# One chunk per turn, and seven products for blocks 2 and 3 too, in a fused recurrence and two-layer kernel

## Chip, cores, metric

One core of one Trainium2 chip (trn2). The metric is device time in microseconds, the median of several executions. "Span" is the time from the first to the last instruction in the profile; the device time of an execution is 1.7 to 3.3 us longer than its span.

## The reference

```python
f = lower_bound + (1 - lower_bound) * sigmoid(f_logit)      # [4, 6144, 256]
for t in range(6144):
    h = f[:, t] * h + (1 - f[:, t]) * x[:, t];  y[:, t] = h
h1, h2 = y @ w1, y @ w2                                     # 24576 tokens, 256 -> 1024
out = maximum(h1, h2) @ w_out                               # 1024 -> 256
```

Results are float32. The kernel works in fp16 with float32 accumulation.

## The kernel before

Tokens are cut into 48 *blocks* of 512. Blocks 0 to 3 are fetched singly and turned (transposed) by TensorE. All later tokens come in *chunks* of 1024, two blocks: GpSimd's queue fetches a chunk of f and of x into scratch memory in HBM, converted to fp16, and the sync queue then transposes the scratch into SBUF by DMA. Chunk p+2 feeds *pair* p (blocks 2p and 2p+1), p = 2 to 23.

Per block there are a gate (sigmoid, ScalarE), decay, drive and two scans (VectorE), then two layers. The maximum is written h1 + relu(h2 − h1), so the *first layer* is y · (w2 − w1) with a ReLU (16 matmuls 512 wide, ScalarE's ReLU after each four), and the *second layer* contracts 8 pieces of the ReLU with w_out and 2 pieces of y with w1·w_out: 40 matmuls 256 wide. From pair 2 on, the second layer of two blocks is one product of 2 x 2 quarters and is done with seven products instead of eight: 140 matmuls 128 wide, at the price of four sums on VectorE. These products of pair p−1 run between the first-layer matmuls of pair p.

```python
def cross(*cs):                       # transposes of one or more chunks, then the next fetch
    if len(cs) > 1:                   # wait until the last chunk is in scratch
        nc.sync.dma_start(out=seen[:], in_=scratch[1][cs[-1] % NSCR][CH - 1 : CH, 0:16])
    for c in cs:
        for s in range(2):            # f, x
            dst = inpool.tile([P, KC, CH], HALF, name=("fT", "xT")[s])
            nc.sync.dma_start_transpose(out=dst[:], in_=scratch[s][c % NSCR][:])
            held[c, s] = dst
    pool_waits(held[cs[-1], 0][:, 0, 0:1])     # a one-column copy on GpSimd
    if cs[-1] + 1 < NCHUNK:
        for s in range(2):
            fetch(cs[-1] + 1, s)
# ... cut ...
# sevenths(p), all pairs but the last: 7 products of 20 matmuls, banks X, B, E in PSUM
product("X", part(0, 0), plain(0, lo), True);  then(seed("B", "X"))       # ScalarE copies X to B
product("E", sub(1), given(t1), True);         then(snapshot("E", 5))
product("X", sub(2), given(t2));               then(snapshot("X", 2))
product("B", part(0, 1), plain(1, lo));        then(leave("B", ja, lo, None, False))  # ScalarE
product("X", sub(3), given(t3));               then(leave("X", jb, hi, 5, False))     # VectorE adds
product("E", sub(4), plain(1, hi));            then(leave("E", ja, hi, 2, True))      # VectorE adds
product("X", part(1, 1), given(t4));           then(leave("X", jb, lo, None, True))   # X again
# ... cut: steps for blocks 0 and 1 ...
        cross(4, 5)
        # block 0's second layer, turn(2), gate(2), block 1's first layer, then
        turn(turn_steps(3));  gate(3);  early = scan_steps(3)
        for fc in range(FC):                    # block 2, beside block 1's second layer
            first_layer(2, fc);  second_layer(1, fc)
            if fc < 4: early[fc]()
        cross(6)
        for fc in range(FC):                    # block 3, beside block 2's second layer
            first_layer(3, fc);  second_layer(2, fc)
            # gates, decay, drive, scans of pair 2 in between
        for p in range(PAIR0, NPAIR):           # 16 slots a pair
            # block 3's second layer beside pair 2; sevenths(p - 1) from pair 3 on
            if slot == 2 and p + 3 < NPAIR:
                cross(blocks[2 * p + 6][3])
```

Of the kernel before, what the change touches and what calls it, by code (L numbers as in the profile page):

```python
# [14 lines left out]
P = 128  # L15
# [3 lines left out]
def kernel(  # L19
# [123 lines left out]

    def cross(*cs):


        if len(cs) > 1:
            nc.sync.dma_start(
                out=seen[:], in_=scratch[1][cs[-1] % NSCR][CH - 1 : CH, 0:16]
            )  # L150
        for c in cs:
            for s in range(2):
                dst = inpool.tile([P, KC, CH], HALF, name=("fT", "xT")[s])
                nc.sync.dma_start_transpose(out=dst[:], in_=scratch[s][c % NSCR][:])
                held[c, s] = dst
        pool_waits(held[cs[-1], 0][:, 0, 0:1])
        if cs[-1] + 1 < NCHUNK:
            for s in range(2):
                fetch(cs[-1] + 1, s)

# [160 lines left out]
    lbc = const.tile([P, KC], FP32)  # L321
    seen = const.tile([1, 16], HALF)
    waited = const.tile([P, 1], FP32)
# [200 lines left out]
    def sevenths(p):  # L524
# [12 lines left out]
        def then(fn):  # L537
            steps[-1][-1] = fn
# [69 lines left out]
        def given(t):  # L608
            return lambda k: t[:, k, :]

        product("X", part(0, 0), plain(0, lo), True)
        then(seed("B", "X"))
        product("E", sub(1), given(t1), True)
# [16 lines left out]
        else:  # L630
            product("X", sub(2), given(t2))
            then(snapshot("X", 2))
            product("B", part(0, 1), plain(1, lo))
            then(leave("B", ja, lo, None, False))
            product("X", sub(3), given(t3))
# [28 lines left out]
    with tc.manual_schedule():  # L664
# [11 lines left out]
        )  # L676
        for c in range(1, 6):
            for s in range(2):
                fetch(c, s)
# [39 lines left out]
        for step in scan_steps(1):  # L719
            step()  # L720
        cross(4, 5)
        for fc in range(FC):
# [8 lines left out]
        for step in scan_steps(2):  # L731
            step()
        for step in make_sevens():
            step()
        for fc in range(2, FC):
            first_layer(1, fc)
            if fc == 3:
                second_layer(0, 7)
        turn(turn_steps(3))
        gate(3)  # L740
        early = scan_steps(3)
        for fc in range(FC):
            first_layer(2, fc)
            second_layer(1, fc)
            if fc < 4:
                early[fc]()
        cross(6)
        scans = {PAIR0: pair_scans(PAIR0)}
        gates = {0: 0, 1: 1, 4: 2, 5: 3}
        order = {  # L750
            2: ("decay0", "drive0"),
            3: ("scan00",),
            4: ("scan01",),
            6: ("decay1",),
            7: ("drive1",),
        }
        for fc in range(FC):
            first_layer(3, fc)
            second_layer(2, fc)
            if fc in gates:  # L760
                pair_gate(PAIR0, gates[fc])
            for t in order.get(fc, ()):
                scans[PAIR0][t]()

        queue, due = [], 0
        pieces3, piece = (1, 3, 5, 9, 11, 13, 15), 0
        for p in range(PAIR0, NPAIR):
            first = p == PAIR0
            more = p + 1 < NPAIR
            seq = [  # L770
                (27, scans[p]["scan10"]),
                (36, scans[p]["scan11"]),
                (112, lambda: sum3(p)),
            ]
            if more:
                scans[p + 1] = pair_scans(p + 1)
                seq += [
                    (64, scans[p + 1]["decay0"]),
                    (66, scans[p + 1]["drive0"]),
                    (70, scans[p + 1]["scan00"]),  # L780
                    (84, scans[p + 1]["scan01"]),
                    (131, scans[p + 1]["decay1"]),
                    (133, scans[p + 1]["drive1"]),
                ]
            if not first:
                seq += [
                    (9, lambda: sum1(p - 1)),
                    (18, lambda: sum2(p - 1)),
                    (50, lambda: sum4(p - 1)),
                ]  # L790
                queue += sevenths(p - 1)
            seq.sort(key=lambda e: e[0])
            gates = {4: 0, 6: 1, 12: 2, 14: 3} if more else {}
            for slot in range(2 * FC):
                first_layer(2 * p + slot // FC, slot % FC)
                if first and slot in pieces3 or p == PAIR0 + 1 and slot == 1:
                    second_layer(2 * PAIR0 - 1, piece)
                    piece += 1
                if p > PAIR0 + 1 or (p == PAIR0 + 1 and slot >= LAG):
                    due += NSEV / (2 * FC)  # L800
                    while due >= 1:
                        due -= 1
                        queue.pop(0)()
                if slot == 2 and p + 3 < NPAIR:
                    cross(blocks[2 * p + 6][3])
                if slot in gates:
                    pair_gate(p + 1, gates[slot])
                while seq and seq[0][0] < (slot + 1) * 9:
                    seq.pop(0)[1]()
# [38 lines left out]
```

## Time and profile before

| | |
|---|---|
| median, range | 379.66 us, 379.19 to 379.68 |
| span | 377.7 us |
| TensorE, VectorE, ScalarE busy | 97%, 90%, 80% |
| a pair in the steady state | 14.70 us, all of it TensorE; VectorE 14.0 |
| loop fetch, transpose, fetch | 14.6 us a chunk (mean between transposes, chunks 8 to 25) |

A group of lines in the profile carries the source line of a helper: L441/L435 is the first layer, L650/L647/L651 the seven products, L487/L481 the plain second layer, L506/L500 the sums, L230/L225 the scans, L285/L280 the gates, L568/L562 an addition that empties a PSUM bank, each first in the kernel before and then in the changed one.

### The profile page before, as it was taken

The page shows a single profiled execution, that of the slowest core. Times are in us where ns is not written, and L with a number is a line of the kernel's source. Part 1 is how long each engine was busy: PE and PEld are TensorE (multiplying, and loading weights), DVE is VectorE, ACT ScalarE, POOL GpSimd, SP SyncE. Part 2 cuts the span into 40 slices and gives each one's busy share as a digit, 9 for nine tenths or more (in the row PEclk, how much of TensorE's full clock was granted, in tenths as well). Part 3 has the DMA queues.
Part 4 walks back from the last instruction along what each step waited for, and adds up shares of the span by engine and source line. Part 5 has one row for each costly group of instructions (what it writes and reads, how often), then busy time and mean ns, then how long its engine had stood idle before and what let it go on. Part 6 is the DMA issues. An engine that isn't in the chain of part 4 may idle for free.

```text
span 377.7 us, 9593 instructions
## 1 busy us (share of the span) xinstructions
PE 367.9 (97%) x4136; PEld 279.8 (74%) x4136; DVE 338.7 (90%) x410; ACT 302.4 (80%) x410; POOL 35.6 (9%) x79
## 2 busy tenths in 40 slices
PE   5999999999999999999999999999999999999994
PEld 3777767777777777777777777777777777777784
DVE  4796789999999999999999999999999999999772
ACT  5865897888888798888888887887988888889752
POOL 1500101110101101101201201011011001010000
PEclk9999999999999999999999999999999999999999
DMA  7996979998999999999999899999899899980223
GB/s 254 246 223 131 309 143 214 227 193 189 273 134 257 223 184 266 222 184 225 203 200 301 208 161 254 147 247 274 132 263 279 134 241 221 185 282 3 112 113 114
DMA packets 104813, 77.17 MB, mean 204 GB/s; under 512 B 93570, under 2 KB 95618, under 8 KB 104066
## 3 DMA queue, kind: packets, MB, share of 16 engines
q1 hardware_dynamic: 101538, 51.19, 60.5%
q0 software_dynamic: 2544, 25.17, 34.7%
q8 instruction: 32, 0.52, 0.6%
q10 hardware_dynamic: 688, 0.20, 0.2%
q14 instruction: 11, 0.09, 0.1%
HBM read 53.48 MB, written 48.23 MB: 269 GB/s over the span
## 4 chain that ended last, share of the span: by engine, by line
PE 94%; DVE 3%; DMA 1%; issue 0%; SPq 0%; ACT 0%; DVEq 0%
PE ps L650 44%; PE dT L441 43%; PE ps L487 5%; DMA osb<-in_x_dram 1%; DVE S L506 1%; PE ps L180 1%; DVE r L230 1%; DVE r L264 1%; PE ps L397 0%; DVE v L223 0%; DVE osb L568 0%; DVE osb L496 0%; PE ps L137 0%; DVE osb L589 0%; PE ps L383 0%
## 5 line engine op out<-in xcount | busy, mean ns | idle before, releaser
L449 ACT ACTIVATE r<-dT 128x1024 f16<-128x1024 f32 x192 | 195.9, 1023 | 53.4 <-PE dT L441 53.2
L441 PE MATMUL dT<-r,wd 128*128 128x512 f16 x768 | 225.5, 379 | 0.4 <-DVE r L230 0.2
L650 PEld LDWEIGHTS <-S 128*128 128x128 f16 x1760 | 115.5, 101 | 37.6 <-issue 0.5
L650 PEld LDWEIGHTS <-r 128*128 128x128 f16 x1320 | 90.9, 101 | 36.8 <-issue 0.2
L230 DVE TENSOR_TENSOR_SCAN r<-ff,r,v 128x512 f16<-128x512 f16 x88 | 108.2, 1269 | 0.8
L650 PE MATMUL ps<-t,S 128*128 128x128 f16 x1320 | 101.6, 219 | 0.0
L506 DVE TENSOR_TENSOR S<-r 128x2560 f16<-128x2560 f16 x44 | 65.3, 1485 | 14.5 <-ACT r L449 14.4
L441 PEld LDWEIGHTS <-wd 128*128 128x128 f16 x768 | 67.6, 113 | 5.2 <-DVE wd L365 1.2
L650 PE MATMUL ps<-wob,r 128*128 128x128 f16 x704 | 69.9, 219 | 0.0
L506 DVE TENSOR_TENSOR S<-r,S 128x2560 f16<-128x2560 f16 x44 | 64.8, 1473 | 0.0
L285 ACT ACTIVATE u<-fT 128x512 f16<-128x512 f16 x88 | 56.0, 637 | 1.3 <-DMA fT<-scr 1.3
L213 DVE TENSOR_SCALAR ff<-u,nom 128x512 f16<-128x512 f16 (+1 forms) x98 | 31.5, 344 | 8.5 <-ACT u L285 3.7
L650 PE MATMUL ps<-w,r 128*128 128x128 f16 x176 | 38.5, 219 | 0.0
L348 POOL CAST waited<-fT 128x1 f32<-128x1 f16 x21 | 8.8, 418 | 282.8 <-DMA fT<-scr 282.8
L650 PE MATMUL ps<-t,r 128*128 128x128 f16 x430 | 34.1, 219 | 0.1
L568 DVE TENSOR_TENSOR osb<-ps,sn 128x512 f32<-128x512 f32 x44 | 30.1, 683 | 3.2 <-PE ps L650 3.2
L650 PE MATMUL ps<-wob,S 128*128 128x128 f16 x352 | 32.6, 219 | 0.0
L223 DVE TENSOR_TENSOR v<-u,xT 128x1024 f16<-128x1024 f16 x44 | 30.0, 682 | 0.0
L556 ACT COPY sn<-ps 128x512 f32<-128x512 f32 x44 | 25.8, 587 | 2.4 <-PE ps L650 2.4
L566 ACT COPY osb<-ps 128x512 f32<-128x512 f32 x43 | 25.0, 582 | 0.8 <-PE ps L650 0.8
L487 PEld LDWEIGHTS <-r 128*128 128x128 f16 x160 | 16.0, 101 | 6.6
L650 PE MATMUL ps<-w,S 128*128 128x128 f16 x88 | 19.3, 219 | 0.0
(58 smaller groups left out, 131.9 us busy)
## 6 DMA issues: line engine op xcount, KB each, us to landing
out_dram<-osb SPq DMA_DIRECT2D x46, 512.0 KB, 3.8
scr<-in_f_logit_dram POOLq DMA_DIRECT2D x22, 512.0 KB, 7.9
scr<-in_x_dram POOLq DMA_DIRECT2D x22, 512.0 KB, 10.5
r<-in_moe_w_dram SPq DMA_DIRECT2D x4, 512.0 KB, 6.9
fT<-in_f_logit_dram POOLq DMA_DIRECT2D x3, 256.0 KB, 7.9
xT<-in_x_dram POOLq DMA_DIRECT2D x3, 256.0 KB, 8.5
out_dram<-osb SPq DMA_DIRECT2D x3, 256.0 KB, 2.6
osb<-in_f_logit_dram SPq DMA_DIRECT2D x2, 256.0 KB, 4.5
```

Source lines behind the costliest of these rows:

```text
L213: nc.vector.tensor_scalar(out=ff[:, h, cols], in0=u[:, h, cols], scalar1=nom[:, h : h + 1], scalar2=1.0, op0=ALU.mult, op1=ALU.add,)
L223: nc.vector.tensor_tensor(out=like(v[:, :, cols], xT), in0=like(u[:, :, cols], xT), in1=xT, op=ALU.mult,)
L230: nc.vector.tensor_tensor_scan(out=y_of(j, h), data0=ff[:, h, o : o + TB], data1=v[:, h, o : o + TB], initial=0.0 if t0 == 0 else y_of(j - ...
L285: nc.scalar.activation(out=mids[p + NBLK, "u"][:, h, cols], in_=held[c, 0][:, h, cols], func=AF.Sigmoid, scale=-1.0,)
L441: nc.tensor.matmul(dT[:, fc % 2, :], lhsT=wd[:, kc, unit_cols(fc)], rhs=y_of(j, kc), start=(kc == 0), stop=(kc == KC - 1),)
L449: nc.scalar.activation(out=rts[j, k][:, g - 1 : g + 1, :].rearrange("p q (i m) -> p q i m", m=P), in_=dT[:].rearrange("p q (m i) -> p q i ...
L487: nc.tensor.matmul(ps[:, r, :], lhsT=left, rhs=right, start=(s == 0 and r == 0), stop=(s == n - 1 and r == 1), skip_group_check=True,)
L506: nc.vector.tensor_tensor(out=t[:], in0=a, in1=b, op=op)
L556: nc.scalar.copy(out=t[:], in_=bank[b][:])
L566: nc.scalar.copy(out=dst, in_=bank[b][:])
L568: nc.vector.tensor_tensor(out=dst, in0=bank[b][:], in1=snap[name][:], op=ALU.add)
L650: nc.tensor.matmul(bank[b][:, i, :], lhsT=a[:, k, cols], rhs=w, start=fresh, stop=after is not None, skip_group_check=True,)
```

## The change

Intent: 80 plain matmuls fewer for 140 short ones (the last two blocks with plain second layers join the scheme of the others), one kind of turn for all chunks, and block 3's turn moved forward so that its scans are early.

```diff
-    def cross(*cs):                    # with the wait on "seen"
+    def cross(c):                      # one chunk: two transposes, wait, next fetch
-        for c in range(1, 6):          # chunks fetched ahead
+        for c in range(1, 5):
-        cross(4, 5)
+        cross(4)
+        begin = p == PAIR0 - 1                          # blocks 2 and 3
         product("X", part(0, 0), plain(0, lo), True)
-        then(seed("B", "X"))
+        then(snapshot("X", 1) if begin else seed("B", "X"))
-            product("B", part(0, 1), plain(1, lo))
-            then(leave("B", ja, lo, None, False))
+            product("B", part(0, 1), plain(1, lo), begin)
+            then(leave("B", ja, lo, 1 if begin else None, False))
             if fc == 3:
                 second_layer(0, 7)
-        turn(turn_steps(3))            # after block 1's first layer
-        gate(3)
+                turn(turn_steps(3))    # within block 1
+                gate(3)
+        for step in scan_steps(3) + make_sevens():      # weight differences moved here
+            step()
         for fc in range(FC):
             first_layer(2, fc)
-            second_layer(1, fc)
+            if fc % 2: second_layer(1, fc // 2)
-        cross(6)
+        cross(5)
         for fc in range(FC):
             first_layer(3, fc)
-            second_layer(2, fc)
+            if fc % 2: second_layer(1, 4 + fc // 2)
+            if fc == 5: sum3(1)
-        gates = {0: 0, 1: 1, 4: 2, 5: 3}                # of pair 2, in block 3
+        gates = {0: 0, 2: 1, 4: 2, 6: 3}
         for p in range(PAIR0, NPAIR):
+            late = p <= PAIR0 + 1                       # pairs 2 and 3
-                    (64, scans[p + 1]["decay0"]),
+                    (80 if late else 64, scans[p + 1]["decay0"]),   # drive, scans alike
-            gates = {4: 0, 6: 1, 12: 2, 14: 3}
+            gates = {6 if late else 4: 0, 8 if late else 6: 1, 12: 2, 14: 3}
-            # sevenths(p - 1) from pair 3 on
+            # sevenths(p - 1) from pair 2 on
-                if slot == 2 and p + 3 < NPAIR:
-                    cross(blocks[2 * p + 6][3])
+                if slot == 2 and p + 2 < NPAIR:
+                    cross(blocks[2 * p + 4][3])
```

More of the change, by code (lines that the diff above doesn't have):

```diff
@@ L142, in first_turn @@
             raws[k, s] = dst[:].rearrange("p k i m -> p k m i")
-    def cross(*cs):
-        if len(cs) > 1:
-            nc.sync.dma_start(
-                out=seen[:], in_=scratch[1][cs[-1] % NSCR][CH - 1 : CH, 0:16]
-            )
-        for c in cs:
-            for s in range(2):
-                dst = inpool.tile([P, KC, CH], HALF, name=("fT", "xT")[s])
-                nc.sync.dma_start_transpose(out=dst[:], in_=scratch[s][c % NSCR][:])
-                held[c, s] = dst
-        pool_waits(held[cs[-1], 0][:, 0, 0:1])
-        if cs[-1] + 1 < NCHUNK:
-            for s in range(2):
-                fetch(cs[-1] + 1, s)
+    def cross(c):
+        for s in range(2):
+            dst = inpool.tile([P, KC, CH], HALF, name=("fT", "xT")[s])
+            nc.sync.dma_start_transpose(out=dst[:], in_=scratch[s][c % NSCR][:])
+            held[c, s] = dst
+        pool_waits(held[c, 0][:, 0, 0:1])
+        if c + 1 < NCHUNK:
+            for s in range(2):
+                fetch(c + 1, s)
     def turn_steps(j):
@@ L321 @@
     lbc = const.tile([P, KC], FP32)
-    seen = const.tile([1, 16], HALF)
     waited = const.tile([P, 1], FP32)
@@ L732 @@
             step()
-        for step in make_sevens():
-            step()
         for fc in range(2, FC):
@@ L738 @@
                 second_layer(0, 7)
-        turn(turn_steps(3))
-        gate(3)
-        early = scan_steps(3)
+                turn(turn_steps(3))
+                gate(3)
+        for step in scan_steps(3) + make_sevens():
+            step()
         for fc in range(FC):
             first_layer(2, fc)
-            second_layer(1, fc)
-            if fc < 4:
-                early[fc]()
-        cross(6)
+            if fc % 2:
+                second_layer(1, fc // 2)
+        cross(5)
         scans = {PAIR0: pair_scans(PAIR0)}
-        gates = {0: 0, 1: 1, 4: 2, 5: 3}
+        gates = {0: 0, 2: 1, 4: 2, 6: 3}
         order = {
-            2: ("decay0", "drive0"),
-            3: ("scan00",),
-            4: ("scan01",),
-            6: ("decay1",),
-            7: ("drive1",),
+            3: ("decay0", "drive0", "scan00", "scan01"),
+            7: ("decay1", "drive1"),
         }
@@ L758 @@
             first_layer(3, fc)
-            second_layer(2, fc)
+            if fc % 2:
+                second_layer(1, 4 + fc // 2)
             if fc in gates:
@@ L763 @@
                 scans[PAIR0][t]()
+            if fc == 5:
+                sum3(1)
         queue, due = [], 0
-        pieces3, piece = (1, 3, 5, 9, 11, 13, 15), 0
         for p in range(PAIR0, NPAIR):
@@ L769 @@
             more = p + 1 < NPAIR
+            late = p <= PAIR0 + 1
+            if more:
+                scans[p + 1] = pair_scans(p + 1)
             seq = [
@@ L775 @@
             if more:
-                scans[p + 1] = pair_scans(p + 1)
                 seq += [
-                    (64, scans[p + 1]["decay0"]),
-                    (66, scans[p + 1]["drive0"]),
-                    (70, scans[p + 1]["scan00"]),
-                    (84, scans[p + 1]["scan01"]),
+                    (80 if late else 64, scans[p + 1]["decay0"]),
+                    (82 if late else 66, scans[p + 1]["drive0"]),
+                    (86 if late else 70, scans[p + 1]["scan00"]),
+                    (100 if late else 84, scans[p + 1]["scan01"]),
                     (131, scans[p + 1]["decay1"]),
@@ L784 @@
                 ]
-            if not first:
-                seq += [
-                    (9, lambda: sum1(p - 1)),
-                    (18, lambda: sum2(p - 1)),
-                    (50, lambda: sum4(p - 1)),
-                ]
-                queue += sevenths(p - 1)
+            seq += [
+                (9, lambda: sum1(p - 1)),
+                (18, lambda: sum2(p - 1)),
+                (50, lambda: sum4(p - 1)),
+            ]
+            queue += sevenths(p - 1)
             seq.sort(key=lambda e: e[0])
-            gates = {4: 0, 6: 1, 12: 2, 14: 3} if more else {}
+            gates = {6 if late else 4: 0, 8 if late else 6: 1, 12: 2, 14: 3}
             for slot in range(2 * FC):
                 first_layer(2 * p + slot // FC, slot % FC)
-                if first and slot in pieces3 or p == PAIR0 + 1 and slot == 1:
-                    second_layer(2 * PAIR0 - 1, piece)
-                    piece += 1
-                if p > PAIR0 + 1 or (p == PAIR0 + 1 and slot >= LAG):
+                if p > PAIR0 or slot >= LAG:
                     due += NSEV / (2 * FC)
@@ L803 @@
                         queue.pop(0)()
-                if slot == 2 and p + 3 < NPAIR:
-                    cross(blocks[2 * p + 6][3])
-                if slot in gates:
+                if slot == 2 and p + 2 < NPAIR:
+                    cross(blocks[2 * p + 4][3])
+                if more and slot in gates:
                     pair_gate(p + 1, gates[slot])
```

## The prediction

> **What bounds the kernel now.** I read the page first: busy shares, then the chain of waits.
>
> ```profile
> PE 367.9 (97%) x4136; PEld 279.8 (74%) x4136; DVE 338.7 (90%) x410; ACT 302.4 (80%) x410; POOL 35.6 (9%) x79
> PE 94%; DVE 3%; DMA 1%; issue 0%; SPq 0%; ACT 0%; DVEq 0%
> ```
>
> TensorE carries 94% of the chain, and VectorE is close behind at 90%. An average hides stages, so next I cut the execution into stretches: blocks 2 and 3 (first layers beside plain second layers), pair 2 (blocks 4 and 5, beside block 3's second layer), pair 3 (the first with seven products beside it), and two later pairs.
>
> ```profile
> core 0: us, PE busy (x) PEld busy (x) DVE busy (x) ACT busy (x) POOL busy (x), PEclk, DMA share, GB/s
> 28.06:43.70 15.64, 15.64 (x116) 11.63 (x113) 10.02 (x15) 10.78 (x14) 0.77 (x3) 1.00 0.86 169
> 43.70:54.50 10.80, 10.80 (x70) 7.16 (x69) 9.86 (x14) 9.71 (x13) 0.55 (x1) 1.00 0.96 221
> 54.50:69.20 14.70, 14.46 (x162) 10.74 (x160) 14.36 (x19) 12.09 (x17) 1.16 (x3) 1.00 1.06 206
> 69.20:83.90 14.70, 14.70 (x175) 11.18 (x173) 14.47 (x18) 12.41 (x18) 2.52 (x6) 1.00 1.03 195
> 83.90:98.60 14.70, 14.70 (x176) 11.17 (x174) 13.91 (x17) 12.41 (x18) 0.09 (x1) 1.00 1.09 202
> ```
>
> A pair runs in 16 slots, each with two 512-wide first-layer matmuls and, in the steady state, 8 or 9 of the 140 product matmuls, from slot 2 on for the first pair that has them. From pair 3 on, a pair lasts 14.70 us, all TensorE; VectorE has 14.0 us of work in it, so it can win back only 0.7 us a pair when late. In the stretch of blocks 2 and 3 it has 5.6 us to spare. In the first pair with seven products TensorE idles 0.24 us. Why is in VectorE's and TensorE's order of time:
>
> ```profile
> 56.08 0.69 DVE L496 COPY osb<-ps 128x512 f32<-128x512 f32 x1 [0.30 <-PE ps L487]
> 56.68 1.48 DVE L506 TENSOR_TENSOR S<-r 128x2560 f16<-128x2560 f16 x1
> 58.08 1.48 DVE L506 TENSOR_TENSOR S<-r,S 128x2560 f16<-128x2560 f16 x1
> 59.48 2.45 DVE L230 TENSOR_TENSOR_SCAN r<-ff,r,v 128x512 f16<-128x512 f16 x2
> ```
>
> ```profile
> 58.29 0.50 PE L650 MATMUL ps<-t,S 128*128 128x128 f16 x6
> ...
> 61.99 0.38 PE L441 MATMUL dT<-r,wd 128*128 128x512 f16 x1 [0.24 <-DVE r L230]
> ```
>
> Sum 1 ends at 58.1 and the first product that reads it starts at 58.29: just in time. The second scan of block 7 ends 0.24 us late for its first layer. So even before, entry to the seven products is where VectorE touches the path.
>
> **What the Trainium skill says.** "TensorE: Matmul & The Clock Gate", section "Wait — 56ns, not 53.3ns?": warm matmuls follow each other at N ÷ 2.4 GHz plus about 2.5 ns, 55.6 ns for N = 128 and 215.7 for 512. The trace agrees: a slot of two 512-wide matmuls takes 0.43 us, nine 128-wide ones 0.50 us, five 256-wide ones 0.55 us (109 ns each). "VectorE: DVE Perf Modes", section "The perf-mode tier table (the rule you actually need)": tensor_tensor runs at 2x from 16-bit SBUF, at 1x with a PSUM operand. The trace agrees: a sum of 2560 fp16 columns takes 1485 ns, an addition of 512 out of PSUM 683 ns. "DMA: Bandwidth & Descriptors", section "Anatomy of one DMA — SWDGE (gpsimd) path": most of a transfer's fixed cost is completion after the last byte, heaviest when HBM is written. It agrees: the last burst of chunk 5's x is over by about 29.6, its landing is seen at 32.6.
>
> **The change part by part.** I use spacings in the trace: sum 1.40, pair of scans 2.38, decay (both halves) 0.53, drive 0.60 to 0.71 (1.25 out of PSUM), addition or copy out of PSUM 0.60, ReLU 0.92, gate 0.53.
>
> (1) TensorE's work. Out: the plain second layers of blocks 2 and 3, 2 x 40 matmuls x 109 ns = 8.72 us. In: 7 products x 20 matmuls x 55.7 ns = 7.80 us. Net -0.92 us, all on the path. The products no longer fall in the blocks 2/3 stretch, which shrinks to 32 x 0.216 + 40 x 0.109 = 11.3 us, from 15.6; they fall beside pair 2, which grows from 10.8 to about 13.7 us, with 0.97 us left for pair 3.
>
> (2) VectorE's work. Out: 4 plain copies. In: 4 sums (5.6 us) and 3 additions (block B is begun with a snapshot, so it needs one more). Net +5.0 us, and 1.94 us of weight differences move behind the scans of block 3, in a stretch that is 4.4 us shorter.
>
> (3) Block 3's turn inside block 1. Its gate (0.92) now stands on ScalarE ahead of the ReLUs of block 1's last two pairs of columns. The ReLU of columns 4 and 5 then ends about 28.5; block 2's first matmul, due at 28.2, needs its PSUM buffer. Cost about +0.35 us.
>
> (4) Chunks. Chunk 5 is no longer fetched ahead, nor waited for. Before, the transposes of chunk 4 started only when chunk 5 was in, and ScalarE waited for them:
>
> ```profile
> 32.59 0.30 SPq L148 DMA_DIRECT2D seen<-scr  x1
> 32.99 1.69 SPq L154 DMA_TRANSPOSE fT<-scr  x1
> ```
>
> ```profile
> 37.89 0.63 ACT L285 ACTIVATE u<-fT 128x512 f16<-128x512 f16 x1 [1.33 <-DMA fT<-scr]
> ```
>
> The trace has chunk 4's f landed at 25.3 (issued 12.6, 12.7 us to landing), x at 27.8; with 4.8 us for a transpose, fT is there by 30 to 34. The gate needs it at 34.9. Chunk 5: fetch issued about 31, in at 39 to 42, transposed by 44 to 46; its gate is due at about 46.5. So the transfers are hidden, with 2 to 3 us to spare there. Later the loop fetch, transpose, fetch took 14.51 us a chunk (first columns 99.3 to 331.6 in 16), under TensorE's 14.7, and gates used chunks 4 to 8 us after landing; the new loop runs about 1.5 us later. Cost 0.
>
> (5) Walk of the queues from block 2 on, each engine in order. TensorE begins block 2 at 28.6, block 3 at 34.2, and would be ready for pair 2 at 39.85. ScalarE: last ReLU of block 2 at 33.9 to 34.85 (TensorE releases it), gate 35.4, ReLU 36.4, second gate 36.9. VectorE idles for that from 35.0 (block 3's gate 27.4, then 0.53 + 1.25 + 2.38 to the end of its scans at about 31.7, differences 33.7, copy of block 1 when TensorE is through with it, 35.0), then decay 37.2, drive 37.9, scans of block 4 at 40.3. TensorE waits **0.45 us**. VectorE goes on: sum 3 41.7, copy 42.3, decay and drive 43.4, sum 1 44.8, sum 2 46.2, scans of block 5 48.6. TensorE from 40.3: two slots of 0.43, two of 0.93, the rest of product X: it wants sum 1 at 43.6 and waits **1.25 us**. Then to slot 8 at 48.1, where block 5's second scan makes it wait **0.45 us** more. After that the postponed decay and scans for block 6 are done at about 54.3, before pair 2 ends at 55.9; pair 3's sum 1 (59.5, wanted 59.8) and second scan (63.3, wanted 63.5) just hold. From pair 4 on it is the old steady state.
>
> Sum: -0.92 (products) - 0.24 (pair 3's old wait) + 0.35 + 0.45 + 1.25 + 0.45 = **+1.3 us**; 379.66 + 1.3 = 381.0.
>
> **Rivals.** *The saving comes through.* If the walk is pessimistic, since I add VectorE's spacings without gaps but with all dependencies at their worst, what is left is -0.92 - 0.24: 378.5. For it: VectorE has 5.6 us of slack in the stretch that loses time, and the new late places for block 6's decay and scans (slots 8 to 11) look chosen to spread this load. Against it: the slack lies before the gates, where VectorE has nothing it may do. *The transfers become the bound.* One chunk's lead less, and a loop of 14.5 us beside pairs of 14.7: if chunk 5's transpose takes the 8.9 us that one later transpose took, its gate waits on ScalarE and holds the ReLUs; 1 to 2 us more: 382 to 383. Against it: only one gate in the whole trace waited for a transfer (1.33 us). *ScalarE becomes the bound in block 3:* four ReLUs and four gates are 5.8 us in a stretch of 5.63; this is in the walk already and could cost 0.3 more.
>
> **Range and chances.** The walk says 381.0, the rival without waits 378.5; I think the walk much likelier, and shade it slightly to 380.7. Ends: full saving, 378.5, and a transfer wait on top, 382.5. A change of 2% is 7.6 us, more than any path here gives.
>
> **What would show it.** Right: the plain second-layer matmuls fall from 160 to 80 and 128-wide products rise by 140; TensorE has idle time before the first layer of block 4 and of block 5 (released by scans) and before the first product on sum 1 (released by the sum), some 2 us in all near 40 to 48 us; pairs 4 to 23 still take 14.7 us; no gate waits for a transpose over 1 us. Wrong: no idle on TensorE in that stretch (378.5), or ScalarE gates waiting for transposes in pairs 2 to 5, or a pair period other than 14.7.

## The result

The changed kernel takes 383.24 us (382.61 to 384.12, 4 runs) against 379.67 of before in the same rounds: +3.6 us. A ratio is the mean of one kernel's fast runs over the mean of the other's fast runs of the same rounds, so not quite the ratio of the medians: 1.0099, interval 1.0076 to 1.0121. The predicted 380.7 had the right side and less than a third of the size, and 383.24 lies above the range's end of 382.5. Two later measurements of the same kernel gave 382.51 and 383.38.

The page after, busy line and chain:

```profile
PE 368.0 (96%) x4196; PEld 279.2 (73%) x4196; DVE 343.9 (90%) x413; ACT 304.7 (80%) x414; POOL 43.7 (11%) x80
DMA 67%; PE 18%; DVE 6%; issue 4%; ACT 2%; POOL 2%; SPq 0%; POOLq 0%; DVEq 0%
```

Before, TensorE carried 94% of the chain. Now a chain of transfers carries 67%. That is a warning to read on, not a verdict: the chain is followed back from the end, and one late transfer near the end, released by the transfer before it, pulls the whole series in. The stretches say more. These are, in the columns that the prediction shows, blocks 2 and 3, pair 2, pair 3 and pair 4, and one stretch late in the execution:

```profile
28.38:40.22 11.84, 11.65 (x74) 7.72 (x74) 9.65 (x18) 10.49 (x13) 1.41 (x3) 1.00 1.08 225
40.22:55.00 14.78, 13.19 (x144) 9.60 (x144) 14.34 (x17) 10.96 (x15) 1.44 (x4) 1.00 1.11 211
55.00:70.00 15.00, 14.10 (x164) 10.59 (x163) 13.76 (x17) 11.77 (x17) 1.89 (x3) 1.00 0.98 196
70.00:84.70 14.70, 14.40 (x170) 10.93 (x169) 14.61 (x17) 11.94 (x18) 1.51 (x3) 1.00 1.04 214
...
276.10:290.80 14.70, 13.79 (x158) 10.29 (x156) 14.46 (x17) 11.13 (x16) 2.96 (x3) 1.00 1.06 216
```

TensorE is busy 13.19 of 14.78 us in pair 2, 14.10 of 15.00 in pair 3, 14.40 of 14.70 in pair 4, and short again by 0.91 near 280 us. Its order of time, all pieces from block 2 on that waited (in brackets how long, and for whom; the view gives no bracket to waits under 0.15 us):

```profile
28.38 1.02 PE L435 MATMUL dT<-r,wd 128*128 128x512 f16 x4 [0.27 <-ACT r L443]
40.22 1.24 PE L435 MATMUL dT<-r,wd 128*128 128x512 f16 x5 [0.18 <-DVE r L225]
44.73 0.51 PE L647 MATMUL ps<-t,S 128*128 128x128 f16 x6 [1.29 <-DVE S L500]
48.50 0.38 PE L435 MATMUL dT<-r,wd 128*128 128x512 f16 x1 [0.30 <-DVE r L225]
56.59 0.27 PE L647 MATMUL ps<-t,r 128*128 128x128 f16 x2 [0.90 <-DVE osb L562]
71.77 0.27 PE L647 MATMUL ps<-t,r 128*128 128x128 f16 x2 [0.30 <-DVE osb L562]
...
278.96 0.27 PE L647 MATMUL ps<-t,r 128*128 128x128 f16 x2 [0.84 <-DVE osb L562]
```

The first four are the four that the prediction walked to, in its order and at its places. The other three were not in it: the last product of a pair accumulates into bank X again, and may not start before VectorE has read bank X out.

**A bracket is too short by 0.16 us.** A first-layer matmul is drawn 379 ns long although the next starts after 216, and a short one 219 ns long, the next 56 after. So each gap hides 0.163 us under a drawn end, and each of these waits costs its bracket plus 0.16. The first six: 3.24 + 6 x 0.16 = 4.20 us.

**A sum that closes.** To leave out the start-up (17.95 to 18.68 us in these profiles) and the last store's completion, I measure the *body*: from the first matmul of block 0's second layer to the end of the last VectorE instruction. Before: 355.04 us. Changed: 359.54 in the first profile, 357.91 in both later ones. With the two terms of the prediction that hold (−0.92 us of matmuls, −0.40 for the old wait of 0.24 + 0.16) and the six waits: −0.92 − 0.40 + 4.20 = +2.88; measured 357.91 − 355.04 = **+2.87**. The first profile has 1.63 us more, all after 260 us, where ScalarE's gates, and once VectorE's drive, wait for transposes:

```profile
269.07 0.63 ACT L280 ACTIVATE u<-fT 128x512 f16<-128x512 f16 x1 [0.68 <-DMA fT<-scr]
...
273.86 0.69 DVE L218 TENSOR_TENSOR v<-u,xT 128x1024 f16<-128x1024 f16 x1 [1.85 <-DMA xT<-scr]
...
285.08 0.63 ACT L280 ACTIVATE u<-fT 128x512 f16<-128x512 f16 x1 [0.91 <-DMA fT<-scr]
```

The drive's wait for the x half of its chunk is the one that reaches TensorE most: VectorE then works without a pause up to the addition that TensorE waits 0.84 us for near 279 us.

So there is an *early* loss of 2.87 us, the same in all three profiles of this kernel, and a *late* one that comes and goes.

Why VectorE is behind in pair 2 shows in its own order of time, with the transfers long in:

```profile
34.22 0.69 DVE L490 COPY osb<-ps 128x512 f32<-128x512 f32 x1 [0.61 <-PE ps L481]
35.24 0.35 DVE L208 TENSOR_SCALAR ff<-u,nom 128x512 f16<-128x512 f16 x1 [0.34 <-ACT u L280]
36.71 0.35 DVE L208 TENSOR_SCALAR ff<-u,nom 128x512 f16<-128x512 f16 x1 [1.12 <-ACT u L280]
...
54.47 1.47 DVE L500 TENSOR_TENSOR S<-r 128x2560 f16<-128x2560 f16 x1
55.85 0.69 DVE L562 TENSOR_TENSOR osb<-ps,sn 128x512 f32<-128x512 f32 x1
```

Between 33.4 and 36.7 it idles 2.07 us, 1.46 of them for the first two gates of pair 2; after that it works with one pause of 0.41 us until 64.7. The last two lines are the wait for bank X: the addition that empties it stands behind sum 3 and ends at 56.54; TensorE starts at 56.59.

### The profile page after: what moved, and what is told of

It reads as the page before. It is cut to its first block, busy times and chain, and to the rows that moved or that the text cites. A ratio compares the mean times of both kernels' runs of the same rounds, so it can differ in the third digit from the quotient of the medians.

```text
span 382.2 us, 9721 instructions
## 1 busy us (share of the span) xinstructions
PE 368.0 (96%) x4196; PEld 279.2 (73%) x4196; DVE 343.9 (90%) x413; ACT 304.7 (80%) x414; POOL 43.7 (11%) x80
## 4 chain that ended last, share of the span: by engine, by line
DMA 67%; PE 18%; DVE 6%; issue 4%; ACT 2%; POOL 2%; SPq 0%; POOLq 0%; DVEq 0%
DMA fT<-scr 35%; DMA scr<-in_f_logit_dram 31%; PE ps L647 8%; PE dT L435 8%; POOL waited L342 2%; DVE r L225 2%; DVE S L500 1%; PE ps L481 1%; ACT r L443 1%; DMA osb<-in_f_logit_dram 1%; DVE v L218 1%; ACT u L280 1%; DVE r L259 1%; DVE ff L208 1%; PE ps L175 0%
## 5 line engine op out<-in xcount | busy, mean ns | idle before, releaser
L647 PEld LDWEIGHTS <-S 128*128 128x128 f16 x1840 | 120.7, 101 | 40.9 <-DVE S L500 1.6
L647 PEld LDWEIGHTS <-r 128*128 128x128 f16 x1380 | 95.1, 101 | 41.0 <-issue 2.6
L647 PE MATMUL ps<-t,S 128*128 128x128 f16 x1380 | 106.3, 219 | 1.3 <-DVE S L500 1.3
L500 DVE TENSOR_TENSOR S<-r 128x2560 f16<-128x2560 f16 x46 | 68.3, 1485 | 12.3 <-ACT r L443 12.1
L647 PE MATMUL ps<-wob,r 128*128 128x128 f16 x736 | 73.1, 219 | 0.0
L500 DVE TENSOR_TENSOR S<-r,S 128x2560 f16<-128x2560 f16 x46 | 67.9, 1476 | 0.0
L342 POOL CAST waited<-fT 128x1 f32<-128x1 f16 x22 | 18.0, 820 | 290.1 <-DMA fT<-scr 290.1
L647 PE MATMUL ps<-w,r 128*128 128x128 f16 x184 | 40.3, 219 | 0.0
L562 DVE TENSOR_TENSOR osb<-ps,sn 128x512 f32<-128x512 f32 x47 | 32.1, 684 | 3.2 <-PE ps L647 3.2
L544 ACT COPY ps<-ps 128x512 f32<-128x512 f32 x22 | 12.5, 570 | 3.3 <-PE ps L647 0.6
```

The lines of the kernel that those rows point to most:

```text
L342: nc.gpsimd.tensor_copy(out=waited[:], in_=t)
L500: nc.vector.tensor_tensor(out=t[:], in0=a, in1=b, op=op)
L562: nc.vector.tensor_tensor(out=dst, in0=bank[b][:], in1=snap[name][:], op=ALU.add)
L647: nc.tensor.matmul(bank[b][:, i, :], lhsT=a[:, k, cols], rhs=w, start=fresh, stop=after is not None, skip_group_check=True,)
```

## The experiments

In all of them the working is that of the changed kernel unless said otherwise, all results are correct unless said otherwise, and "before" ran in the same rounds. Bodies are from the one profiled execution of each. Runs e1 to e4, e5 to e8, e9 to e12 and e13 to e16 were each on another chip.

| run | what | median us | before | ratio, interval | body us | loop us |
|---|---|---|---|---|---|---|
| before | | 379.66 | | | 355.04 | 14.60 |
| changed, first | | 383.24 | 379.67 | 1.0099, 1.0076–1.0121 | 359.54 | 15.34 |
| e1 | transposes a pair ahead | 382.76 | 379.50 | 1.0088, 1.0074–1.0103 | 357.90 | 14.36 |
| e2 | bank B seeded (wrong result) | 382.48 | 379.50 | 1.0078, 1.0061–1.0096 | 357.31 | 15.20 |
| e3 | block 3 turned after block 1 | 382.15 | 379.50 | 1.0071, 1.0058–1.0084 | 357.48 | 14.79 |
| e4 | order of pair 2 recast | 383.68 | 379.50 | 1.0107, 1.0093–1.0122 | 357.95 | 15.02 |
| e5 | gates of pair 2 early | 380.63 | 379.60 | 1.0033, 1.0017–1.0049 | 355.65 | 14.82 |
| e6 | no late places | 381.43 | 379.60 | 1.0055, 1.0043–1.0067 | 356.94 | 14.56 |
| e7 | chunk part alone, on before | 379.93 | 379.60 | 1.0010, 0.9998–1.0022 | 355.00 | 15.00 |
| e8 | e1 + e3 + e5 + e6 | 381.26 | 379.60 | 1.0053, 1.0040–1.0066 | 356.44 | 14.15 |
| e9 | e1 + e5 + e6 + sum 3 later | 379.45 | 379.67 | 0.9995, 0.9974–1.0017 | 354.14 | 14.42 |
| e10 | e5 + e6 + sum 3 later | **378.59** | 379.67 | 0.9970, 0.9953–0.9987 | 354.14 | 14.54 |
| e11 | changed, again | 382.51 | 379.67 | 1.0073, 1.0056–1.0090 | 357.91 | 14.87 |
| e12 | e2 with an unused buffer (wrong result) | 382.99 | 379.67 | 1.0073, 1.0051–1.0095 | 358.15 | 14.89 |
| e13 | loop opened | 420.08, one fast run 408.33 | 379.64 | – | – | 16.51 |
| e14 | stores from ScalarE's queue | 395.80 | 379.64 | 1.0417, 1.0382–1.0451 | 373.20 | 14.83 |
| e15 | e10 with the loop opened | 425.81, one fast run 390.80 | 379.64 | – | – | 19.09 |
| e16 | changed, a third time | 383.38 | 379.64 | 1.0095, 1.0082–1.0108 | 357.91 | 14.95 |

Medians of one kernel move by up to 0.9 us, so differences of a few tenths are read from bodies and named waits, not from medians. Three profiles (e2, e3, e12) have a last store that landed 3.8 to 4.2 us after the last VectorE instruction instead of 2.5 to 2.6, so that the span ends 5.6 to 6.0 us after it instead of 4.3 to 4.5; that is 1.2 to 1.6 us of one execution's time that no edit explains. Expectations that start from the first measurement also contain its late loss: e3 and e6 came out 0.8 and 1.1 us under theirs, but 0.36 and 1.08 under e11, close to what their bodies say (0.43 and 0.97).

**The theories.** V: TensorE's waits are one VectorE backlog, which starts where VectorE idles for the gates; L: the loop fetch, transpose, fetch became slower because each transpose is issued right behind two stores. Rival S: each wait is a matter of its own.

### e1: transposes a pair ahead

```diff
         cross(5)
+        cross(6)
-                if slot == 2 and p + 2 < NPAIR:
-                    cross(blocks[2 * p + 4][3])
+                if slot == 2 and p + 3 < NPAIR:
+                    cross(blocks[2 * p + 6][3])
```

> The changed kernel with the transposes of each chunk issued one pair earlier in the sync queue again (chunk 6 right behind chunk 5, then the chunk of pair p+3 in pair p, as before); nothing else. Theory L (the loop fetch - transpose - fetch became slower than a pair because each transpose is now issued behind two fresh stores, and one chunk's lead less exposes it): the loop's mean period falls from 15.3 us to 14.6 to 14.8, first-column landings from 7.1 to about 6 us, no gate after pair 6 waits for a transpose, and the time falls by 0.8 to 1.0 us, to about 382.4. Rival R1 (the loop is slow for another reason, such as the phase of VectorE's sums against GpSimd's copy): the period stays above 15.1 and the time at 383.2.

The loop's period fell to 14.36 us, no gate waited for a transpose, and all six early waits stood unchanged: body 357.90. Four of five executions lay within 382.69 to 382.83. This first divided the loss: 2.86 early, the rest late. Against the first measurement the time is 0.5 lower, against e11 0.25 higher, so the gain in time is not shown.

### e2: bank B seeded as in all other pairs

```diff
-        begin = p == PAIR0 - 1
+        begin = False
```

> The changed kernel with the products of blocks 2 and 3 begun as those of all other pairs (bank B seeded by a ScalarE copy, and left by a ScalarE copy, no snapshot and no addition on VectorE): 0.60 us of VectorE work less between 52 and 54 us. Theory V (from the first scan of block 4 until pair 4 VectorE works without a break and TensorE's waits are one backlog): the wait for bank X at 56.6 falls from 0.90 to about 0.3 and that of pair 4 from 0.30 to 0; the time falls by 0.6 to 0.9, to about 382.5. Rival S (each wait is its own dependency, bank X waits for the sum ahead of it in any case): time unchanged within 0.2.

The wait for bank X fell from 0.90 to 0.31 and the body by 0.60, the length of the addition taken from VectorE: as theory V had it for this wait. The wait of pair 4 stayed at 0.30, against it. **The result is wrong** (relative error 0.088). It tells why the change has a special beginning; see below.

### e3: block 3 turned after block 1

```diff
                 second_layer(0, 7)
-                turn(turn_steps(3))
-                gate(3)
+        turn(turn_steps(3))
+        gate(3)
```

> The changed kernel with block 3 turned and gated after all of block 1's first layer, as before. Both theories: the wait of 0.27 us shown (0.43 with what a matmul's modelled end hides) before block 2's first layer goes. Theory V: TensorE is then 0.4 us early but VectorE is not, as it waits for the gates of pair 2, which TensorE's progress releases: these come 0.4 earlier too, so everything moves 0.3 to 0.4: about 382.9. Rival S: the same 0.4. If the gate's being 0.9 later holds VectorE's scans of block 3, the gain is lost: 383.2 or more.

The first wait is gone and all others are as they were; the body is 0.43 us shorter, 0.27 + 0.16. So this part of the change costs 0.43 by itself.

### e4: order of pair 2 recast

```diff
-            if fc == 5:
-                sum3(1)
+        # in pair 2: sum 1, scans of block 5, sum 3, sum 2, sum 4
         then(snapshot("X", 1) if begin else seed("B", "X"))
+        if begin:
+            product("B", part(0, 1), plain(1, lo), True)
+            then(leave("B", ja, lo, 1, False))
         product("E", sub(1), given(t1), True)
```

> The changed kernel with the order of pair 2 recast: product B of blocks 2 and 3 stands second, sum 3 and sum 2 come after block 5's scans, so that no product and no first layer of pair 2 waits long for VectorE (the waits of 1.29 and 0.30 us shown there, some 1.9 with what modelled ends hide, should fall to about 0.8). VectorE's work is the same. Theory V (one VectorE backlog): the time won comes back as longer waits for bank X at the end of pair 2 and in pair 3; net gain at most 0.4: 382.8 to 383.3. Rival S (each wait its own cost): the gain of 1.1 to 1.3 stays: about 382.0.

Net gain none: body 357.95 against 357.91. In TensorE's order of time the wait of 1.29 us for sum 1, the one of 0.30 for the scans and the one of 0.90 for bank X are gone, and these stand in their place:

```profile
49.00 0.23 PE L651 MATMUL ps<-t,S 128*128 128x128 f16 x1 [1.21 <-DVE S L500]
53.06 0.55 PE L651 MATMUL ps<-t,S 128*128 128x128 f16 x7 [1.48 <-ACT sn L550]
```

All five waits make 4.25 us with the hidden ends, against 4.20 of six. That the sums are so equal is partly chance. The first new wait is for VectorE, but the second is the recast's own: with product B moved forward, two products into bank X stand next to each other, and the second has to wait until ScalarE has copied bank X out (52.43 to 53.01). So e4 alone doesn't decide against rival S. An estimate from its trace speaks for V: without that wait, 1.64 us with the hidden end, TensorE would have come to the last product into bank X at about 55.4, and VectorE, which worked without a pause from 37.1 us on, had the bank read out only at 56.6. About 1.2 of the 1.64 us would have come back.

### e5: the gates of pair 2 early

```diff
+        scans = {PAIR0: pair_scans(PAIR0)}
         for fc in range(FC):
             first_layer(2, fc)
+            if fc in (3, 5):
+                pair_gate(PAIR0, fc // 4)
+            if fc == 5:
+                for t in ("decay0", "drive0", "scan00", "scan01"):
+                    scans[PAIR0][t]()
             if fc % 2: second_layer(1, fc // 2)
         cross(5)
-        gates = {0: 0, 2: 1, 4: 2, 6: 3}
-        order = {3: ("decay0", "drive0", "scan00", "scan01"), 7: ("decay1", "drive1")}
+        gates = {0: 2, 2: 3}
+        order = {3: ("decay1", "drive1")}
```

> The changed kernel with the four gates of pair 2 brought forward: the first two stand within block 2 on ScalarE (its transpose landed at 30 us), so that block 4's decay, drive and scans follow the weight differences on VectorE without a break, and the other two early in block 3. No work is added or removed. Theory V (TensorE's waits of pairs 2 and 3 are one VectorE backlog, and it stems from the 2.07 us that VectorE idled between 33.4 and 36.7 us, mostly for the gates): the waits of 0.18, 1.29 and 0.30 us vanish, that for bank X at 56.6 falls below 0.3, and the time falls by 2.5 to 3.0, to 380.2 to 380.8. Rival A (ScalarE then holds the ReLUs of block 2, and TensorE waits for PSUM buffers instead): at most 1.5 is won: 381.7 or more.

No instruction was added or removed, and 380.63 us came out. TensorE's order of time, all that waited from block 2 on:

```profile
28.36 1.02 PE L435 MATMUL dT<-r,wd 128*128 128x512 f16 x4 [0.27 <-ACT r L443]
54.31 0.27 PE L647 MATMUL ps<-t,r 128*128 128x128 f16 x2 [0.90 <-DVE osb L562]
69.50 0.27 PE L647 MATMUL ps<-t,r 128*128 128x128 f16 x2 [0.30 <-DVE osb L562]
```

The three waits of pair 2 are gone, and the body is shorter by 2.26: 0.18 + 1.29 + 0.30 + 3 x 0.16 = 2.25. The cause of these three is thus VectorE's idle time before the gates. But the two waits for bank X stand to the hundredth, so they are no part of that backlog: theory V was too wide.

### e6: no late places

```diff
-            late = p <= PAIR0 + 1
+            late = False
```

> The changed kernel without the later places that it gives the gates, decay and scans of the next pair in pairs 2 and 3 (the places of all other pairs instead). Theory V: the late gates made VectorE idle 0.41 us at 50.5 and 1.21 us at 66.3; without that the wait for bank X in pair 4 (0.30 shown) goes and the one at 56.6 falls from 0.90 to about 0.5: 0.5 to 0.9 us faster than the changed kernel, about 382.5. Rival (the later places were needed: decay and scans ahead of what TensorE waits for): waits in pair 2 grow, 383.2 or more.

Bank X: 0.90 became 0.39, and 0.30 went; the body is shorter by 0.97 (0.51 + 0.30 + 0.16). So the late places make most of these two waits: the late second gate holds VectorE (0.41 us at 50.5, 1.21 at 66.3), and everything behind it, with the addition that frees bank X at the end, keeps its distance from that gate however early VectorE was before. The remaining 0.39 belongs to the place of sum 3, not to the gates: in e10 below, with early gates and no pause on VectorE, the addition ends at 52.09 us and the product that needs it starts at 52.99; an estimate with sum 3's 1.40 us still ahead of the addition makes it some 0.5 us late, again 0.39 shown. No run has e5 and e6 without the moved sum 3.

### e7: the chunk part alone, put into the kernel before

> The kernel before with the chunk part of the change alone (chunk 5 not fetched ahead, one chunk per turn, each chunk's transposes one pair later in the sync queue). Theory L (that order makes the loop slower: stores just ahead of each transpose): loop period 14.9 to 15.4 against 14.6 before, gates wait for transposes late in the execution, time 379.5 to 380.5, with a wider spread than before. Rival R2 (the loop is slowed by what the rest of the change does, the order alone is harmless): period 14.6, no late waits, 379.3 to 379.6.

(The edit is the `cross`, `fetch` and `seen` part of the change and nothing else.) Body 355.00 against 355.04, no late wait in the profile, loop 15.00. The median is 0.33 higher, with an interval of the ratio that includes 1. The chunk part alone has no loss that this study can show, though its loop was slower in the one profile. Period and time are thus as theory L had them, the late waits are not.

### e8: four mendings at once

> The changed kernel with four mendings at once: transposes one pair ahead again (as e1), block 3 turned after block 1 (as e3), gates of pair 2 early (as e5), no late places (as e6). Theory V and L together: no TensorE wait above 0.3 us is left from block 2 on, and what remains is the arithmetic of the change, -0.92 us of matmuls and the old 0.24 us wait (0.4 with what a matmul's modelled end hides): 378.1 to 378.7, faster than both kernels. If waits of 1 us or more remain, the theory of one backlog is incomplete: 379.3 or more.

It failed: 381.26. Two of TensorE's waits:

```profile
44.15 0.51 PE L647 MATMUL ps<-t,S 128*128 128x128 f16 x6 [1.56 <-DVE S L500]
...
55.51 0.27 PE L647 MATMUL ps<-t,r 128*128 128x128 f16 x2 [0.39 <-DVE osb L562]
```

and VectorE's, before the decay of block 3:

```profile
29.21 0.62 DVE L208 TENSOR_SCALAR ff<-u,nom 128x512 f16<-128x512 f16 x2 [2.74 <-ACT u L202]
```

Turning block 3 later makes VectorE wait 2.74 us for its gate, 0.89 in the changed kernel. In e3 that lateness was hidden, as VectorE had to wait for the gates of pair 2 anyway; with these early, it is the backlog's new source. A mending that gains alone can lose in company. The sum still closes: −0.92 − 0.40 + (1.56 + 0.30 + 0.39 + 3 x 0.16) = +1.41; measured 356.44 − 355.04 = +1.40.

### e9 and e10: mended, with block 3 turned within block 1

e10 is e5 and e6 and one line more; e9 has the order of e1 as well.

```diff
-                (112, lambda: sum3(p)),
+                (126 if first else 112, lambda: sum3(p)),
```

> The changed kernel (block 3 still turned within block 1) with the early gates of e5, no late places (e6), the transposes a pair ahead (e1), and sum 3 of pair 2 behind the addition that frees bank X. Theory: the run with all mendings failed only because turning block 3 late made VectorE wait 2.74 us for its gate and put the backlog back; with the turn kept, only the wait of 0.27 us before block 2 is left. Arithmetic: -0.92 (matmuls) - 0.40 (old wait) + 0.43 = -0.9: 378.5 to 379.0, 0.7 to 1.0 under the kernel before. Rival (waits move on once more, to the next sum or bank): 379.5 or more, with a new wait over 0.3 us between 40 and 75 us.

> As e9_mended, but with the change's own order of chunks (one per turn, transposes one pair later). Theory L: its loop has a period of 14.8 to 15.3 us against 14.1 to 14.6 in e9_mended; in some executions gates late in the kernel wait for transposes: median 0.2 to 0.8 above e9_mended, and a wider spread. Rival: no difference (within 0.15).

Both bodies are 354.14, 0.90 us *under* the kernel before; the arithmetic said −0.92 − 0.40 + 0.43 = −0.89. Of all waits from block 2 on, one is left, here of e10:

```profile
28.10 1.02 PE L435 MATMUL dT<-r,wd 128*128 128x512 f16 x4 [0.27 <-ACT r L443]
```

e10 takes 378.59 us, 1.1 under before in the same rounds (0.9970, interval 0.9953 to 0.9987). It is the fastest version, with the change's own order of chunks. e9 was expected to be the better one and was not: 379.45, with a spread of 378.78 to 381.01 whose longer executions were not profiled. What theory L says of the time has this against it.

### e11 and e16: the changed kernel again

> The changed kernel once more, as the yardstick of this call: 383.0 to 383.5 by its first runs. If late waits for transposes are what varies, its executions lie 382.6 to 384.2 and the fastest near the median of e1 (382.7).

> The changed kernel as yardstick of this call. Theory O: 382.5 plus what late waits add on this chip: 382.4 to 383.5; in its profile the loop's period and late waits go together: none below 14.9 us, some above 15.1.

The median of e11, 382.51, is under the 383.0 to 383.5 that was expected. In both profiles the body is 357.91, with the six early waits and no late one, at loop periods of 14.87 and 14.95. So the early loss repeats exactly, and the late one is not always there. That some period above 15.1 would show in e16 was not borne out; nor do period and late waits go together, as e12 has a period of 14.89 and two late gates (0.76 us at 195.6, 0.23 at 239.4), and e4 a period of 15.02 and none.

### e12: the seed in another bank

```diff
+                if p == PAIR0 - 1:
+                    ps_o.tile([P, TB // P, P], FP32, name="ps")   # unused
                 open_bank(b)
```

> e2 again (bank B seeded by a ScalarE copy for blocks 2 and 3), with one unused PSUM buffer taken first, so that the seeded bank is one that the second layer of block 1 had written in full, and not one last written by transposes. Theory W (the seed was lost because a matmul that doesn't start a group adds only where a matmul had written before): the result is now correct, and the time that of e2: 0.6 to 0.7 below the changed kernel. Rival (the seed races with the product): still wrong.

Wrong again, with the same relative error to all digits. The test did not test: in the built program the seeded bank has the same PSUM address in e2 and e12, that of a buffer last written by block 3's transposes, since an unused buffer comes free at once. Theory W is neither shown nor refuted. The Trainium skill supports it ("PSUM — Partial Sum Buffer", section "The four PSUM rules": a ScalarE write doesn't set the bits by which a matmul decides between adding and overwriting). That the seed of blocks 2 and 3 is lost is the reading that fits two equal errors; no run proves it.

### e13 and e15: the loop opened

```diff
-        pool_waits(held[c, 0][:, 0, 0:1])
+        if c > 4:
+            pool_waits(held[c - 1, 0][:, 0, 0:1])
```

> The changed kernel, but GpSimd waits for the previous chunk's transpose instead of this chunk's before it fetches the next chunk, so that fetch and transpose of different chunks overlap; scratch reuse still waits for its own transpose. Theory O (the late waits of the first measurement came from the closed loop fetch - transpose - fetch, whose period of 15.3 us exceeded a pair's 14.7): transposes then come as early as the sync queue's place allows, no gate waits for one, and the time is what the early part alone costs, 379.6 + 2.9 = 382.5, every execution within 0.6 of it but for the longer last store that some executions have (1.2 to 1.6). Rival (fetch and transpose in flight together slow each other so that landings double): late waits in the profile, 383 or more.

> The fastest version so far (e10: early gates, no late places, sum 3 behind bank X's addition, the change's own order of chunks) with the opened loop of e13. If its loop was no longer a limit, as its profile showed no wait for a transpose, the time stays at 378.6 within 0.3; if some of its unprofiled executions had late waits, the spread narrows and the median falls to 378.3.

Far off: 408.33 and 390.80 us in the one fast run of each (granted clock 0.983 and 0.988); the other five of each are marked slow (over 1.5% above their own fastest, and the profiled ones with a granted clock of 0.979 and 0.942), and I compare none of them. The rival named with e13 was right, and worse than it said. In the profile (a slow run, so only the direction counts), transfers, with the median from issue to landing at the end of each line, first e13, then the changed kernel:

```profile
scr<-in_f_logit_dram POOLq DMA_DIRECT2D x22, 512.0 KB, 9.7
fT<-scr SPq DMA_TRANSPOSE x22, 15.5
```

```profile
scr<-in_f_logit_dram POOLq DMA_DIRECT2D x22, 512.0 KB, 6.3
fT<-scr SPq DMA_TRANSPOSE x22, 7.4
```

With a fetch running beside it a transpose landed after twice the time, and the loop's period rose from 14.95 (e16) to 16.51 us, so the overlap cost more than it gave. GpSimd's one-column copy, which looks like a needless wait, keeps the two apart.

### e14: stores from ScalarE's queue

```diff
-        (queue or nc.sync).dma_start(
+        (queue or nc.scalar).dma_start(
```

> The changed kernel with its output stores issued from the ScalarE queue, so that no store stands ahead of a transpose in the sync queue. Theory L (a transpose lands late because it is issued right behind stores): landings of the first half fall from about 7 us to below 6.2, the loop's period to 14.6 or less, no late waits; but ScalarE pays the issue, some 1 us a pair of the 2.3 that it has free: 382.3 to 383.0. Rival (all share the same 16 engines, so the place in the queue does not matter): landings stay near 7 and the period at 14.8 to 15.3.

The rival's reading of the loop holds: landings of 7.1 us and a period of 14.83, with no store ahead of any transpose in its queue. Theory L, as put, falls. The 16 us are another matter. In the profile the largest part is one wait of 10.8 us of ScalarE's queue, before a ReLU at 73.6 us, for a transpose; ScalarE, held, held TensorE for 10.2. Why that queue waited for a transpose is not shown. The granted clock was 0.980 to 0.985 in the six executions; in the profile it was 0.77 from 60 to 90 us, the stretch with that wait, and 1.00 in the stretches before and after.

## Why the prediction was wrong, point by point

- **TensorE's work, −0.92, and the old wait.** Right, but for the hidden end of the old wait (0.24 in the prediction, 0.40 in the sums): they enter every sum above, and these close within 0.03 us (e5, e6, e8, e10, e11).
- **The four waits of the walk.** Right in cause, order and size: predicted 0.35, 0.45, 1.25, 0.45, in sum 2.50; measured with the hidden ends 0.43, 0.34, 1.45, 0.46, in sum 2.68. Block 3's turn was confirmed alone (e3), and VectorE's idling for the gates as the source of the other three too (e5).
- **The failed step**, word for word: "pair 3's sum 1 (59.5, wanted 59.8) and second scan (63.3, wanted 63.5) just hold. From pair 4 on it is the old steady state." The walk asked of each VectorE instruction whether its *result* would come in time, and never whether its *reading* would free a buffer in time. Bank X must be read out before the pair's last product; that addition stands behind sum 3 in VectorE's queue. The late places, which the prediction took for a help ("look chosen to spread this load"), postpone it. Two terms were missing: 0.90 + 0.16 in pair 3 and 0.30 + 0.16 in pair 4, 1.52 us. e6 took 0.97 of them away with one word; in e9 and e10, where sum 3 stands behind the addition, the rest is gone too. With them the walk gives +2.9, that is 382.5: what e11 measured (382.51), and the end of the range.
- **The transfers, "Cost 0".** Right for chunks 4 and 5, wrong as a whole for the first measurement. The prediction took the loop at 14.51 us a chunk from the old trace, 0.2 under a pair, and concluded that it would stay ahead. In the first profile it took 15.34, above a pair's 14.7: the lead of a transpose's landing over its first gate fell from 5.0 us at chunk 8 to 0.0 at chunk 20, and 1.63 us were lost. In the two later profiles of the same kernel it took 14.87 and 14.95, also above a pair, but the lead only fell from 3.8 to 3.2 and from 3.9 to 2.1 by chunk 25 (at least 1.3 in between), so that no gate waited. A margin of 0.2 us a pair was no ground for a zero.
- **What stays open.** Why the loop's period differs between executions. Two parts are seen in the first profile against before: the first half of a chunk landed in 7.1 us on average instead of 6.1 (chunks 8 to 25; its fetch was shorter by 0.8), and GpSimd's copy took 0.82 us instead of 0.42. In the three profiles with the old order of chunks among the mended kernels (e1, e8, e9) the period was 14.15 to 14.42, in those with the new one 14.54 to 15.34; but neither e7 nor e10 shows a cost in time for it, and the stores' place in the queue is not the reason (e14). How much of the 383.24 and 383.38 is late waits and how much longer last stores can't be told, as the unprofiled executions leave no trace.

## What to carry to other kernels

When a queue falls behind, ask of each entry not only who needs its result but who needs the buffer that it reads. If several waits in a row have one idle stretch upstream, work on that stretch: reordering behind it (e4) won nothing, while bringing the gates forward (e5) won 2.3 us. And before a "needless" wait between transfers is taken out, find what it keeps apart.

## What the Trainium skill lacked or had wrong

- "Advanced Engine Details and Errata", section "X-Bar Transpose (TRN2)", says that transposing DMAs are as fast as regular ones. In the changed kernel the x half of a chunk, transposed second, landed in 4.8 us (median), close to the 4.4 of a plain store of the same 512 KB; the f half, transposed first, took 7.4. No run times one alone, so this doesn't contradict the page. What no page gives is a time for a transpose with a fetch into HBM scratch beside it: 15.5 us for the f half (e13, a slow run).
- "GPSIMD Engine Reference", section "1. Specifications", has it that GpSimd shares SBUF interfaces with VectorE instructions that have two SBUF inputs. The trace agrees and adds a size: the copy of one column took 0.18 us when free, and its mean was 820 ns in the changed kernel against 418 before. The copy below began during the sum of 54.47 and ended at 55.98, the sum at 55.94.

```profile
54.89 1.09 POOL L342 CAST waited<-fT 128x1 f32<-128x1 f16 x1 [11.31 <-DMA fT<-scr]
```

- No page gives the 0.16 us by which a matmul's drawn end makes every TensorE gap look shorter (379 ns drawn, 216 from start to start): without it six waits here would be 0.98 us too small in sum.
- No page has the landing of a kernel's last store as a term that varies: it came 2.5 to 2.6 us after the last VectorE instruction in most profiles and 3.8 to 4.2 after it in three (e2, e3, e12).
